# A decode attention kernel: value blocks move from the sync engine's transfer queue to ScalarE's

## The chip, the cores and the metric

The kernel runs on one core of a Trainium2 chip. A core has five engines that run their own instruction streams: TensorE (PE) for matrix products, VectorE (DVE), ScalarE (ACT), GpSimd (POOL) and the sync engine (SP). Transfers between the chip's main memory and the on-chip memory are started by an instruction on SP, ACT or POOL; the data is then moved by 16 DMA engines, which all three share. In the profile the queue that SP fills is called q1, the one that ACT fills q10, and the one that POOL fills q0.

The metric is device time in microseconds (us). Several runs of one kernel are timed without the profiler, and their median counts; one more execution is profiled.

## The reference

The computation is one decode step of a layer: attention with a cache and a small dense network, both on the same normalised input, summed with the input.

```python
xn = layernorm(x)                                   # x: 8 sequences x 512
q = (xn @ wq) -> 32 heads x 128                     # 4 query heads share one key/value head
scores = einsum("bhqd,bhkd->bhqk", q, k) * 128**-0.5   # k_cache: 8 x 8 heads x 8192 x 128
p = softmax(scores)
o = einsum("bhqk,bhkd->bhqd", p, v)                 # v_cache: 8 x 8 heads x 8192 x 128
out = x + o.reshape(8, 4096) @ wo                   # wo: 4096 x 512
        + mish(xn @ w1 + b1) @ w2                   # w1: 512 x 1792, w2: 1792 x 512
```

All numbers are 32-bit. The two caches hold 268 MB each, and every element is used once, so the caches make up nearly all of the 562 MB that the kernel reads.

## The kernel before, in words

The attention is cut into 32 units. A unit `j` is one sequence (`b = j % 8`) and two key/value heads (`m = j // 8`). It needs one block of keys and one block of values; each is 128 partitions x 16384 numbers, that is 64 KB in each partition and 8.39 MB in all. `load_unit` (line 135) starts such a transfer, and `load_q` (line 130) starts one of 2 MB with the part of `wq` that the next eight units need.

All blocks lie in one on-chip array `kv` with room for two and a half blocks: the value block at column 0, and two places for keys (`K_AT`) that overlap by half. Three rules follow for when a transfer may start, and a transfer's instruction waits for them on the engine that issues it:

- The keys of unit j+1 may come when the first half of the scores of unit j is done (`scores(..., 0)`, 32 matmuls of line 330), because that half has used up the columns that the next block overwrites.
- The values of unit j may come when the matmuls of `values(j-1)` (line 392) have used up the value block before.
- The values of the last unit go into a key place, and may come after the first half of the last unit's scores.

Within a unit PE does, in this order: the first half of the scores, the second half, two tiny transposes for the softmax's maximum, then `values(j-1)` of the unit before, and then `turn(j)` (lines 369 and 370), which re-arranges the exponentials for the next unit's `values`. DVE finishes `turn(j)` with transposes and sums (lines 374 and 380). ACT does one exponential per unit (line 361). Some units have more on PE between `values` and `turn`: `turn_act` in unit 2 (line 490), and `project` in units 5, 13 and 21 (lines 265 and 276), which makes the queries of the next group from `wq`. In units 7, 15 and 23 `spread` (line 301) does the rest of that.

Everything stands in the order in which the code writes it. SP issues nearly all transfers, first to last: keys of j+1, values of j, keys of j+2, and so on, with `wq` behind the values of units 4, 12 and 20. Two small gathers of early rows of `w2` (line 516, units 14 and 22) go by POOL's queue. After the loop SP starts `wo` in five transfers into the value place, 2 MB for each of `w_o[0]`, `w_o[1]`, `w_o[2]`, and 1 MB twice for `w_o[3]`, and then the rest of `w2` in four. Meanwhile PE does the last `values`, `outputs` (line 506), and `down` (line 553), and DVE and one last transfer end the kernel.

Of the kernel before, what the change touches and what calls it, by code (L numbers as in the profile page):

```python
# [35 lines left out]
NP = HKV // 2  # L36
# [5 lines left out]
UNITS = NP * B  # L42
# [34 lines left out]
def kernel(  # L77
# [12 lines left out]
    nc = tc.nc  # L90
# [7 lines left out]
    kv = const.tile([P, PLACES], F32, name="kv")  # L98
# [36 lines left out]
    def load_unit(src, j, at):  # L135
        m, b = divmod(j, B)
        lo = (b * HKV + 2 * m) * NH * G
        t = kv[:, at : at + ROW]
        nc.sync.dma_start(
            t,  # L140
            src[lo : lo + NB].rearrange("j p f -> (j p f)").rearrange("(p f) -> p f", p=P),
        )
        return t
# [18 lines left out]
    load_q(0)  # L162
    nc.scalar.dma_start(b1_sb, b1.rearrange("(g f) -> g f", g=B))
    k_t = {0: load_unit(kT, 0, V_AT)}
    w1_t = kv[:, W1_AT : W1_AT + 7168]

# [7 lines left out]
    for g in range(4):  # L174

        src = ident.rearrange("p (c d u g h) -> p d u g c h", c=2, d=2, u=2, g=4)
# [388 lines left out]
    key_weights(0)  # L565
    turn_x()
    k_t[1] = load_unit(kT, 1, K_AT[1])
    find_early()

# [3 lines left out]
    for j in range(UNITS):  # L573
# [3 lines left out]
        k = k_t.pop(j)  # L577
# [3 lines left out]
        if j == UNITS - 1:  # L581
            v_t[j] = load_unit(v, j, K_AT[0])
        elif j > 0:
            k_t[j + 1] = load_unit(kT, j + 1, K_AT[(j + 1) % 2])
# [30 lines left out]


    w_o = [kv[:, 4096 * m : 4096 * (m + 1)] for m in range(NP)]
    for m in range(NP):
        rows = wo[4 * m : 4 * (m + 1)].rearrange("u (k i) f -> (u k) (i f)", i=4)
        step = 4096 if m + 1 < NP else 2048  # L620
        for at in range(0, 4096, step):
            nc.sync.dma_start(w_o[m][:, at : at + step], rows[:, at : at + step])
    w2_rows = w2.rearrange("j p f -> (j p f)")[: P * FU * D].rearrange("(q f) -> q f", q=P)
    w2_t = []
    parts = ((0, 4), (4, 6), (6, 8), (8, 9))
# [65 lines left out]
```

## Time and profile before

| What | Value |
|---|---|
| median of 3 runs (lowest, highest) | 1308.74 us (1308.43, 1309.89) |
| profiled execution, its own time | 1308.41 us |
| span of that execution (first to last instruction) | 1306.6 us |
| PE busy | 995.1 us, 76% |
| DVE busy | 526.4 us, 40% |
| ACT busy | 41.4 us, 3% |
| bytes moved, mean rate over the span | 561.79 MB, 430 GB/s |
| mean granted TensorE clock | 0.878 |

The profiled execution's own time is 1.8 us more than its span, and 0.3 us less than the median. The rate is the sum over all 16 DMA engines. A row of a queue gives its packets, its megabytes, and the time that its packets took as a share of 16 engines' time. In the chain of waits each row is a start, a duration, and who was at work then. In the timeline the part in square brackets is how long the engine had been idle before the row, and for whom it waited.

### The profile page before, as it was taken

Reading aid. Unit: us, or ns where it says so; the run is one execution under the profiler, and the core shown is the slowest. Engines: PE = TensorE matmul, PEld = TensorE weight load, DVE = VectorE, ACT = ScalarE, POOL = GpSimd, SP = SyncE. Lnnn points to the kernel's source line nnn. Section 1 sums busy time; section 2 is a strip of 40 time slices with the busy share of each in tenths; the row PEclk is TensorE's granted clock in tenths of the full one; section 3 lists DMA queues with packets and bytes.
Section 4 is the critical chain, followed back from the end, with each engine's and each line's share of the span. In section 5 each row is a group of like instructions: output and inputs, shape, how many; then the busy total and the mean of one; then the engine's idle time right before and its main releaser. Section 6 shows DMA issues by size and latency. Waiting matters only on the chain.

```text
span 1306.6 us, 11259 instructions
## 1 busy us (share of the span) xinstructions
PE 995.1 (76%) x5046; PEld 336.1 (26%) x5046; DVE 526.4 (40%) x787; ACT 41.4 (3%) x90; POOL 7.8 (1%) x30
## 2 busy tenths in 40 slices
PE   5969977777977678777788777787776787776686
PEld 2324322222322222222222222222222222222221
DVE  4463344432444433244253444413444333444423
ACT  1000000000000000000000000000000000000000
POOL 1000000000000000000000000000000000000000
PEclk9988888798888789888898888798897998888888
DMA  9999999999999999999999999999999999999998
GB/s 405 442 424 440 428 436 432 432 434 434 430 436 426 441 424 444 420 446 418 446 418 446 420 444 422 442 426 438 424 440 430 434 432 434 430 436 428 439 424 356
DMA packets 11743, 561.79 MB, mean 430 GB/s; under 512 B 1464, under 2 KB 1600, under 8 KB 1992
## 3 DMA queue, kind: packets, MB, share of 16 engines
q1 hardware_dynamic: 11376, 559.75, 99.2%
q0 software_dynamic: 288, 1.31, 0.2%
q8 instruction: 39, 0.64, 0.2%
q14 instruction: 8, 0.07, 0.0%
q10 hardware_dynamic: 32, 0.02, 0.0%
HBM read 562.85 MB, written 0.07 MB: 431 GB/s over the span
## 4 chain that ended last, share of the span: by engine, by line
DMA 67%; PE 29%; DVE 3%; ACT 1%; issue 0%; DVEq 0%
DMA kv<-in_kT 34%; DMA kv<-in_v 31%; PE s L330 14%; PE o L392 10%; DMA kv<-in_w 2%; PE x L369 1%; PE x L301 1%; PE m L490 1%; DVE pt L380 1%; PE h L434 0%; PE h L265 0%; PE m L276 0%; ACT qr L304 0%; DVE ws L465 0%; DVE nm L342 0%
## 5 line engine op out<-in xcount | busy, mean ns | idle before, releaser
L330 PE MATMUL s<-kv,wk 128*64 128x512 f32 x2048 | 505.7, 656 | 160.3 <-DMA kv<-in_kT 160.3
L392 PE MATMUL o<-kv,pt 128*32 128x512 f32 x2048 | 264.3, 675 | 45.9 <-DMA kv<-in_v 36.3
L330 PEld LDWEIGHTS s<-kv,wk 128*64 128x64 f32 x2048 | 155.7, 152 | 482.6 <-issue 319.5
L380 DVE TENSOR_REDUCE pt<-tr 64x512 f32<-64x2048 f32 x64 | 241.3, 3771 | 1.5
L342 DVE TENSOR_REDUCE nm<-s 128x1 f32<-128x512 f32 x32 | 22.1, 692 | 335.8 <-PE s L330 335.8
L369 PE MATMUL x<-e,perm 128*128 128x512 f32 x256 | 129.7, 654 | 2.0 <-ACT qr L304 2.0
L392 PEld LDWEIGHTS o<-kv,pt 128*32 128x32 f32 x2048 | 69.0, 122 | 214.6 <-issue 166.3
L400 DVE TENSOR_SCALAR os<-o,isel 128x128 f32<-128x128 f32 x32 | 11.2, 351 | 261.5 <-PE o L392 261.5
L374 DVE STREAM_TRANSPOSE tr<-x 128x512 f32<-128x512 f32 x128 | 78.7, 673 | 0.0
L369 PEld LDWEIGHTS x<-e,perm 128*128 128x128 f32 x256 | 50.2, 206 | 77.9 <-issue 72.2
L313 DVE TENSOR_TENSOR wk<-qr,mask 128x512 f32<-128x512 f32 x64 | 62.9, 1025 | 16.2 <-ACT qr L304 16.2
L361 ACT ACTIVATE e<-s,nmx 128x512 f32<-128x512 f32 x32 | 22.0, 687 | 1076.1 <-DVE nmx L358 1076.1
L402 DVE SCALAR_TENSOR_TENSOR os<-o,isel,os 128x128 f32<-128x128 f32 x96 | 33.7, 351 | 3.4
L343 PE MATMUL m<-ident,nm 128*1 128x128 f32 x32 | 8.7, 273 | 30.5 <-DVE nm L342 30.5
L354 PE MATMUL m<-ident,nx 1*128 1x1 f32 x32 | 7.0, 219 | 24.0 <-DVE nx L350 24.0
L372 DVE RECIPROCAL rt<-m 128x8 f32<-128x8 f32 x32 | 6.6, 208 | 44.5 <-PE m L370 44.5
L409 PE MATMUL m<-hsel,os 128*128 128x8 f32 x64 | 12.6, 270 | 12.3 <-DVE rt L372 12.3
L301 PE MATMUL x<-wk,tr 128*128 128x512 f32 x16 | 13.1, 914 | 10.8 <-DVE wk L296 8.2
L363 DVE TENSOR_SCALAR lsel<-rsel,l 128x8 f32<-128x8 f32 x32 | 7.4, 231 | 30.0 <-ACT e L361 30.0
L343 PEld LDWEIGHTS m<-ident,nm 128*1 128x1 f32 x32 | 2.5, 79 | 58.7 <-DVE nm L342 58.7
L370 PEld LDWEIGHTS m<-lsel,ones 128*128 128x128 f32 x64 | 12.2, 190 | 15.5 <-issue 15.3
L347 DVE TENSOR_REDUCE nr<-m 1x4 f32<-1x64 f32 x64 | 10.9, 206 | 11.7 <-PE m L343 11.7
(114 smaller groups left out, 201.5 us busy)
## 6 DMA issues: line engine op xcount, KB each, us to landing
ws<-in_wq SPq DMA_DIRECT2D x4, 2048.0 KB, 33.8
kv<-in_wo SPq DMA_DIRECT2D x3, 2048.0 KB, 24.0
kv<-in_w SPq DMA_DIRECT2D x1, 3584.0 KB, 34.9
kv<-in_wo SPq DMA_DIRECT2D x2, 1024.0 KB, 30.4
kv<-in_w SPq DMA_DIRECT2D x1, 1024.0 KB, 32.5
kv<-in_w SPq DMA_DIRECT2D x2, 512.0 KB, 28.9
kv<-in_kT SPq DMA_DIRECT2D x32, 29.5
kv<-in_v SPq DMA_DIRECT2D x32, 30.6
```

What stands on the lines that cost most here:

```text
L301: nc.tensor.matmul(X[:, half], pick, r[:, i].rearrange("p i c -> p (i c)"), start=True, stop=True)
L313: nc.vector.tensor_mul(w[:, :, d], q[:, :, d].to_broadcast([P, DI, NH * G, REP]), mask[:, d * NH * G : (d + 1) * NH * G] .rearrange("p (o ...
L330: nc.tensor.matmul(S[64 * c : 64 * (c + 1), :], w[:, i].rearrange("p d k h -> p (d k h)"), kk[:, i, c, :], start=(part == 0 and n == 0), s ...
L342: nc.vector.tensor_reduce(nm, S, axis=AX.X, op=ALU.max, negate=True)
L361: nc.scalar.activation(e, S, AF.Exp, bias=nmx, accum_out=l)
L369: nc.tensor.matmul(X[:, g], perm[:, g], e, start=True, stop=True)
L374: nc.vector.transpose(tr.rearrange("p (l t) c -> p t l c", t=TL)[:, tl], X.rearrange("p g (t q l) -> p t l g q", t=TL, q=PP)[:, tl],)
L380: nc.vector.tensor_reduce(pt8[half, :, :, d * REP : (d + 1) * REP].rearrange("p c y h -> p y c h"), tr[half].rearrange("p y (g c h) -> p y ...
L392: nc.tensor.matmul(O[Q * q : Q * (q + 1), :], pt8[:, c, TL * l : TL * (l + 1), :].rearrange("p t h -> p (t h)"), vt[:, 512 * n : 512 * (n ...
L402: nc.vector.scalar_tensor_tensor(os, O[:, DH * i : DH * (i + 1)], isel[:, i : i + 1], os, op0=ALU.mult, op1=ALU.add)
L409: nc.tensor.matmul(M[:, 168 : 168 + H2], os, hsel, start=True, stop=True)
L490: nc.tensor.matmul(M[:, 256 + i * B : 256 + (i + 1) * B], w, bsel[:, :B], start=True, stop=True)
```

## The change

Values of units 0 to 30 are issued by ACT in place of SP. Keys, `wq`, the values of unit 31, `wo` and `w2` stay with SP. The first two blocks of `wo` become one transfer of 4 MB. No arithmetic is changed.

```diff
@@ load_unit
         t = kv[:, at : at + ROW]
-        nc.sync.dma_start(
+        (nc.scalar if src is v and j + 1 < UNITS else nc.sync).dma_start(
             t,
             src[lo : lo + NB].rearrange("j p f -> (j p f)").rearrange("(p f) -> p f", p=P),
         )
@@ after the loop over the units
     w_o = [kv[:, 4096 * m : 4096 * (m + 1)] for m in range(NP)]
-    for m in range(NP):
-        rows = wo[4 * m : 4 * (m + 1)].rearrange("u (k i) f -> (u k) (i f)", i=4)
-        step = 4096 if m + 1 < NP else 2048
-        for at in range(0, 4096, step):
-            nc.sync.dma_start(w_o[m][:, at : at + step], rows[:, at : at + step])
+    wo_rows = wo.rearrange("(m u) (k i) f -> m (u k) (i f)", m=NP, i=4)
+    nc.sync.dma_start(
+        kv[:, :8192].rearrange("p (m f) -> p m f", m=2),
+        wo_rows[:2].rearrange("m p f -> p m f"),
+    )
+    nc.sync.dma_start(w_o[2], wo_rows[2])
+    for at in (0, 2048):
+        nc.sync.dma_start(w_o[3][:, at : at + 2048], wo_rows[3, :, at : at + 2048])
```

On SP, units 2 to 5: `in_kT` are keys, `in_v` values, `in_wq` the query weights. Before:

```order
L139 DMA kv<-in_kT 128x16384
L139 DMA kv<-in_v 128x16384
L139 DMA kv<-in_kT 128x16384
L139 DMA kv<-in_v 128x16384
L133 DMA ws<-in_wq 128x4096
L139 DMA kv<-in_kT 128x16384
```

And now, from the keys of unit 1 on:

```order
L139 DMA kv<-in_kT 128x16384 x5
L133 DMA ws<-in_wq 128x4096
L139 DMA kv<-in_kT 128x16384 x8
L133 DMA ws<-in_wq 128x4096
L139 DMA kv<-in_kT 128x16384 x8
```

The values are gone from SP's stream, and `wq` now stands directly behind the keys of unit 5 and ahead of those of unit 6, with no block of values between.

On ACT, units 3 to 7: line 361 is a unit's exponential, line 273 a copy in `project`, line 304 one in `spread`. Before:

```order
L361 ACTIVATE e,l<-s,nmx 128x512 x5
L273 COPY e<-h 128x512 x2
L361 ACTIVATE e,l<-s,nmx 128x512 x2
L304 COPY qr<-x_69 128x512 x2
L361 ACTIVATE e,l<-s,nmx 128x512 x6
```

And now:

```order
L361 ACTIVATE e,l<-s,nmx 128x512
L139 DMA kv<-in_v 128x16384
L361 ACTIVATE e,l<-s,nmx 128x512
L139 DMA kv<-in_v 128x16384
L273 COPY e<-h 128x512 x2
L361 ACTIVATE e,l<-s,nmx 128x512
L139 DMA kv<-in_v 128x16384
L361 ACTIVATE e,l<-s,nmx 128x512
L139 DMA kv<-in_v 128x16384
L304 COPY qr<-x_69 128x512 x2
```

Each unit's values now stand behind that unit's exponential and ahead of the copies of `project` and `spread`.

On SP, the end. Before:

```order
L139 DMA kv<-in_v 128x16384 x2
L622 DMA kv<-in_wo 128x4096 x3
L622 DMA kv<-in_wo 128x2048 x2
L628 DMA kv<-in_w 128x2048
L628 DMA kv<-in_w 128x1024 x2
L628 DMA kv<-in_w 128x512
```

And now:

```order
L139 DMA kv<-in_v 128x16384
L619 DMA kv<-in_wo 128x2x4096
L623 DMA kv<-in_wo 128x4096
L625 DMA kv<-in_wo 128x2048 x2
L631 DMA kv<-in_w 128x2048
L631 DMA kv<-in_w 128x1024 x2
L631 DMA kv<-in_w 128x512
```

Of the two last blocks of values one is left on SP, and two transfers of `wo` have become one.

## The prediction

> **What bounds the kernel now.** I read the page first: queues, then chain.
>
> ```profile
> q1 hardware_dynamic: 11376, 559.75, 99.2%
> q0 software_dynamic: 288, 1.31, 0.2%
> ...
> q10 hardware_dynamic: 32, 0.02, 0.0%
> ...
> DMA 67%; PE 29%; DVE 3%; ACT 1%; issue 0%; DVEq 0%
> ```
>
> SP's queue is busy for 99.2% of the time of 16 engines, nearly everything goes through it, and ACT's (q10) is all but unused. The same view for 40 us of the middle:
>
> ```profile
> DMA packets 298, 17.33 MB, mean 433 GB/s; under 512 B 32, under 2 KB 32, under 8 KB 32
> ...
> q1 hardware_dynamic: 296, 17.30, 100.1%
> ```
>
> 296 - 32 = 264 packets carry 17.30 MB, so a packet is 65.5 KB: one partition's row of a block, eight on each engine. 264 packets in 40 us on 16 engines make 2.42 us each, and a block **D = 8 x 2.42 = 19.4 us**. The queue has no gap here. Next the chain at the end:
>
> ```profile
> 1200.40 8.60 PE s L330 x32
> ...
> 1209.02 30.10 DMA kv<-in_kT
> ...
> 1239.16 9.70 PE s L330 x32
> ...
> 1248.88 28.96 DMA kv<-in_v
> ...
> 1277.85 24.61 DMA kv<-in_w
> ...
> 1302.51 0.62 PE h L553 x16
> ```
>
> Keys of unit 31 land at 1239.16, a period of 38.76 us after those of unit 30: exactly two blocks. The chain goes through key loads that were issued about 9 us after a landing and landed 30 us later: 10 us in line, 19.4 us moving. The stream of bytes is the bound, and 10 us of queued work keeps it unbroken.
>
> **Issue times: nothing to win.** The waits of SP's queue and of ACT:
>
> ```profile
> SPq L139 <- PE s L330: 315.7, 32, 19.3
> ...
> SPq L139 <- PE o L392: 253.2, 30, 12.1
> ```
>
> ```profile
> ACT e L361 <- DVE nmx L358: 1076.1, 31, 40.7
> ```
>
> SP waits for PE: for a score half before keys, for `values` before values. PE does these in the order in which SP asks, so none of SP's transfers is held up by its neighbour's wait, and ACT will wait for the same PE instructions. ACT is idle for 1076 us before its exponentials. Behind its new wait stand the next exponential, whose scores PE does after that `values`, and the copies of `project` and `spread`, also later on PE. So the wait on ACT costs nothing; 31 issues of 0.33 us (SP's rows below) hide in that idle time, and without it would cost 10 us. The first values come behind unit 0's exponential:
>
> ```profile
> 29.55 0.33 SPq L139 DMA_DIRECT2D kv<-in_kT  x1
> 44.99 0.33 SPq L139 DMA_DIRECT2D kv<-in_v  x1
> ```
>
> ```profile
> 48.56 0.69 ACT L361 ACTIVATE e<-s,nmx 128x512 f32<-128x512 f32 x1
> ```
>
> That is some 4.3 us later (49.25 against 44.99), while unit 1's keys, asked for at 29.55 behind `wq`, the first keys and `w1`, are still moving: nothing, and 4.3 us if they had already landed.
>
> **What does change: two rings.** Before, a block got all engines until it was through. Now keys and values wait in two queues at once. The one place before where two queues were long in use is POOL's gather in unit 14, 0.92 MB. Its landing, and three stretches of 7.5 us from 565.5 us on:
>
> ```profile
> q0 software_dynamic: 144, 0.92, 6.5%
> ...
> ws<-in_w,idx POOLq DMA_INDIRECT x1, 29.3
> ```
>
> ```profile
> q1 hardware_dynamic: 61, 2.95, 91.0%
> q0 software_dynamic: 61, 0.41, 13.1%
> ```
>
> ```profile
> q1 hardware_dynamic: 46, 3.01, 92.9%
> q0 software_dynamic: 45, 0.25, 7.9%
> ```
>
> ```profile
> q1 hardware_dynamic: 52, 3.41, 104.9%
> q0 software_dynamic: 34, 0.23, 7.3%
> ```
>
> The gather's 16 KB rows, 0.61 us each at a block's rate, are up to eight on an engine: 4.9 us if drained at one go. They trickle through all three stretches instead. Alternating one for one with 64 KB rows takes 8 x (2.42 + 0.61) = 24.2 us, and with some 4 us of start that is the 29.3 us seen. So I take it that the engines alternate between queues row by row, and two blocks then get half the rate each.
>
> The Trainium skill (DMA: Bandwidth & Descriptors, Queues, rings and completion order) says that an engine goes round its queues but drains a whole packet, typically 9 to 17 descriptors, before it switches. By that a block's eight rows on an engine could go as one piece; the stretches above speak against it, and the first rival asks what it would do.
>
> **One period with sharing.** T is the landing of a unit's keys, x the us of the value block that have moved by then. PE's rows in the last unit, all matmuls of the values, PE's clock just after a wait for keys (0.50, the third number from the right), a score half that followed no wait, and SP's last issue:
>
> ```profile
> 1239.16 16.53 PE L330 MATMUL s<-kv,wk 128*64 128x512 f32 x64 [6.14 <-DMA kv<-in_kT]
> ...
> 1258.52 8.51 PE L392 MATMUL o<-kv,pt 128*32 128x512 f32 x64 [0.79 <-DMA kv<-in_v]
> ```
>
> ```profile
> L392 PE MATMUL o<-kv,pt 128*32 128x512 f32 x2048 | 264.3, 675 | 45.9 <-DMA kv<-in_v 36.3
> ```
>
> ```profile
> 690.00:692.00 2.00, 2.00 (x6) 0.70 (x8) 2.00 (x1) 0.00 (x0) 0.00 (x0) 0.50 1.21 524
> ```
>
> ```profile
> 652.40 7.04 PE s L330 x32
> ```
>
> ```profile
> 1303.93 0.35 SPq L652 DMA_DIRECT2D out<-os  x1
> ```
>
> The first half takes 9.2 us (8.60 and 9.70 above). From an issue to its first byte I take 1.6 us: the last transfer was issued at 1303.93, and all of it is over by the span's end, 1306.6, so it is under 2.7. The next keys then start at T + 10.8. PE is ready for `values` at T + 18.6 (1258.52 - 0.79 - 1239.16), which take 8.3 us on average (264.3 / 32).
>
> - Values alone until T + 10.8, then shared: they land at T + 10.8 + 2 x (8.6 - x) = T + 28 - 2x.
> - Their successor starts 9.9 us later. The keys then have 0.9 + x left, and share that: the next x is 0.9 + x. It climbs until the landing meets PE's T + 18.6, at x = 4.7; past that, x' = 38.8 - 27.3 - x with `values` at full clock (7.1 us), so about 5 or 6. Where PE has not idled before the keys its clock is full and the half takes 7.0 us (652.40): the next keys start 2.2 us sooner, and x falls by 1.3 instead.
>
> So x wanders between 0 and 6; I take the middle, **x = 3**. No gap arises in an ordinary unit: the values last past T + 10.8 for x under 8.6. But the cushion, 10 us before, is halved.
>
> **Gaps in long units.** SP's timeline around the issue of unit 2's values and unit 4's keys; the size of a `wq` transfer; and PE's first score matmuls of unit 6, behind `project`:
>
> ```profile
> 123.61 0.33 SPq L139 DMA_DIRECT2D kv<-in_v  x1
> 147.01 0.33 SPq L139 DMA_DIRECT2D kv<-in_kT  x1
> ```
>
> ```profile
> ws<-in_wq SPq DMA_DIRECT2D x4, 2048.0 KB, 33.8
> ```
>
> ```profile
> 255.70 1.12 PE L330 MATMUL s<-kv,wk 128*64 128x512 f32 x2 [4.38 <-DMA kv<-in_kT]
> ```
>
> In unit 2 PE needs 23.4 us from one issue to the other (`turn_act`). All that the engines hold then is that block and what is left of unit 3's keys, which by the sharing is x again: 19.4 + x, so a gap of 4.0 - x, **1.0 us** (0 to 4). In unit 5 `wq` stands ahead of unit 6's keys. Its rows are 16 KB (2048 KB on 128 partitions), eight per engine, and alternate with the 64 KB rows of the values (25% slower: with x = 3, 16.4 x 3.03 / 2.42 = 20.5 us), so the keys start at T + 21. The values' successor starts at 20.5 + 8.3 + 1.6 = T + 30.4; 10 us of keys are left, shared, so they land at T + 50.4, and x is 10 by then: 1.4 over the 8.6 allowed, a gap of 1.4. (PE itself is on time: it had 4.4 us to spare after `project`, and the keys now come later.) The same in units 13 and 21: 3 x 1.4 = **4.2 us**. Sum I = 5.2, from 0 (sharing less even) to 9: a landing waits for the slowest of 16 engines, each up to a packet (2.4 us) off.
>
> **The tail.**
>
> ```profile
> 1281.04 9.19 PE L392 MATMUL o<-kv,pt 128*32 128x512 f32 x64 [9.57 <-DVE pt L380]
> ...
> 1302.51 1.03 PE L553 MATMUL h<-kv,aT 128*8 128x128 f32 x24 [0.48 <-DMA kv<-in_w]
> ```
>
> `values(30)` ends at 1267.03 (1258.52 + 8.51). The rest up to 1306.6 is 39.6 us of PE, DVE and ACT in series, of which only 0.48 waits for a transfer. PE and the stream end together; the slack is half a microsecond. Now the last values share with the block of unit 31. T becomes 1239.1 + I + x, as x us of values went first; `values(30)` ends 28 - 2x + 8.3 later, and the end 39.1 after that: 1314.5 + I - x, against 1306.6 + I for the bytes. At x = 3 it is **+4.9 us**; at 0, +7.9. From x = 4.7 on `values(30)` ends at T + 18.6 + 7.1, and the end is 1303.9 + I + x: +2.0 at 4.7, the least, and +3.3 at 6. The merged `wo` is asked for up to a quarter of `values` (2.1 us) later, behind unit 31's values, which have some 8 us to go: nothing, or 2.1 us without that cover.
>
> Sum on the profiled execution: 1308.4 + 5.2 + 4.9 = **1318.5 us**, its own range 1310.4 (0 and 2.0) to 1325.3 (9 and 7.9). The median lies 0.3 above that execution, which I leave in the rounding.
>
> **The rivals.** For the second, the rate (last number, GB/s) of the stretch in which the tail's bytes come:
>
> ```profile
> 1277.90:1303.20 25.30, 19.66 (x214) 6.44 (x218) 5.70 (x11) 0.58 (x1) 0.00 (x0) 0.85 0.95 397
> ```
>
> - Blocks drained in order of issue (12%): an engine that has begun a block's eight rows finishes them before it looks at the other queue. Then landings, gaps and tail are as before, and so is the time, 1308.7. For it: q1 and q10 were never seen side by side under load. Against: the gather's stretches.
> - Faster (8%): two queues close what q1 leaves open. 99.2 + 0.2 + 0.2% leaves about 0.4%, 5 us, and the start and end hold most of it; the last 25.3 us run at 397 GB/s in place of 433, worth 2.1 us. That gives 1305 to 1306.5. Against: 100.1% in the middle.
> - Sharing with a hidden tail (10%): x ends near 4.7 (+2.0), and `values(31)` finds the full clock, 7.1 us in place of the 9.19 above, which takes those 2.1 us back. Then the gaps alone remain, 1308.4 + 5.2 = 1313.6. For it: x tends to 4.7. Against: `values(31)` waits 9.57 us for DVE in either kernel, and starts cold.
>
> **How the numbers follow.** The forecast has 70%. Some 0.2% (2.6 us) is what a measurement can tell from no change. Forecast and third rival are slower (80%); the first is the same (12%), the second faster (8%). The range runs from 1308, to take in the first rival, to 1326, just past the likeliest one's own end; what it leaves out is the second rival and a tail longer than any x here gives.
>
> **What would show it.** q10 should carry half of the bytes; keys and values should both take well over 30 us from issue to landing; PE's wait for values should grow from 36 us; gaps of 1 to 2 us in the DMA should follow unit 2 and units 5, 13, 21; and at the end PE should no longer wait for `w2`, with `values(30)` ending about 8 to 10 us later. Landings as before in a row would prove the forecast wrong at the sharing; a higher rate than 433 GB/s in the middle would prove the second rival.

## The result and the profile after

The changed kernel takes 1330.7 us (median of four runs, 1327.95 to 1334.29) where the kernel before, beside it, takes 1308.59 (1308.29 to 1309.89). The ratio is 1.017, with a 95% interval from 1.0158 to 1.0183. It is slower, as forecast, but by 22.1 us in place of 10, and beyond the range's end at 1326. The profiled execution is the longest of the four: 1334.29, with a span of 1332.5, 25.9 more than before. All rows of the kernel after come from it.

The page of the kernel after: bytes, queues, the two groups of matmuls, and the median us from issue to landing (these last two rows from the DMA view).

```profile
DMA packets 11728, 561.80 MB, mean 422 GB/s; under 512 B 1448, under 2 KB 1584, under 8 KB 1976
...
q1 hardware_dynamic: 6896, 299.70, 52.7%
q10 hardware_dynamic: 4496, 260.07, 45.4%
...
L330 PE MATMUL s<-kv,wk 128*64 128x512 f32 x2048 | 491.6, 641 | 149.0 <-DMA kv<-in_kT 148.8
L392 PE MATMUL o<-kv,pt 128*32 128x512 f32 x2048 | 265.3, 677 | 103.5 <-DMA kv<-in_v 93.9
...
kv<-in_kT SPq DMA_DIRECT2D x32, 29.8
kv<-in_v ACTq DMA_DIRECT2D x31, 29.5
```

Nearly half of the bytes have moved to q10. The same bytes come at 422 GB/s in place of 430. PE waits 57.6 us more for values (93.9 against 36.3), and 11.5 less for keys (148.8 against 160.3). Keys and values still take only 29.8 and 29.5 us from issue to landing (29.5 and 30.6 before).

**Where the time went.** Busy time by engine in 40 to 1280 us, with the granted clock, the DMA share and the rate as the last three numbers; before, then after:

```profile
40.00:1280.00 1240.00, 950.75 (x4732) 319.85 (x4728) 507.31 (x725) 34.94 (x80) 2.12 (x2) 0.87 1.00 432
```

```profile
40.00:1280.00 1240.00, 919.83 (x4638) 311.86 (x4636) 495.03 (x707) 34.16 (x78) 2.12 (x2) 0.86 0.99 425
```

The middle is 7 GB/s slower, which is 1240 x 7 / 432 = 20 us of the stream's time. In stretches of 100 us of the kernel after, the rate (before: 429 to 436 in every such stretch) is:

| stretch from, us | 40 | 140 | 240 | 340 | 440 | 540 | 640 | 740 | 840 | 940 | 1040 | 1140 |
|---|---|---|---|---|---|---|---|---|---|---|---|---|
| before, GB/s | 436 | 429 | 434 | 432 | 434 | 429 | 435 | 432 | 431 | 434 | 433 | 432 |
| after, GB/s | 419 | 423 | 427 | 430 | 429 | 429 | 431 | 410 | 430 | 423 | 422 | 429 |
| stream time lost, us | 3.9 | 1.4 | 1.6 | 0.5 | 1.2 | 0.0 | 0.9 | 5.1 | 0.2 | 2.5 | 2.5 | 0.7 |

The losses sum to 20.5 us. They are spread over the kernel, most of them in places where the prediction had none. The deepest holes in the same view of the kernel after:

```profile
110.00:120.00 10.00, 10.00 (x48) 3.11 (x46) 0.00 (x0) 0.00 (x0) 0.00 (x0) 0.94 0.84 334
815.00:821.00 6.00, 6.00 (x42) 2.08 (x35) 2.22 (x5) 0.00 (x0) 0.00 (x0) 1.00 0.55 188
1000.00:1005.00 5.00, 5.00 (x26) 1.73 (x24) 3.39 (x2) 0.00 (x0) 0.00 (x0) 1.00 0.77 275
```

PE is busy through all three while the DMA engines are not full: for most of each, the transfers that would fill them are not yet asked for. None of the three is one that the prediction named. PE's rows near the first and the third:

```profile
131.27 9.59 PE L490 MATMUL m<-bsel,ws 128*128 128x8 f32 x42
...
983.79 2.07 PE L301 MATMUL x<-wk,tr 128*128 128x512 f32 x2 [0.67 <-ACT qr L304]
...
993.63 13.95 PE L330 MATMUL s<-kv,wk 128*64 128x512 f32 x64
```

The first hole ends before `turn_act` (line 490) has begun. The gap that the prediction named lies behind `turn_act`, at 150 to 160 us, and left the engines idle for 0.8 us. The third follows the `spread` of unit 23 (line 301), a unit that the prediction did not count among the long ones: PE turned to the keys of unit 24 at 993.63, 8 us after they had landed. Only the second lies in an ordinary unit.

Read packet by packet, the 16 engines stood idle for 12.6 us each between 40 and 1280 us, and for 0.0 in the kernel before. The other part of the loss is in rows that took longer than the usual 2.42 us: the first rows of the blocks add up to 9 us over that on each engine, most of it within 5 us after an idle spell. Why they take longer is not shown.

**One hole, followed.** PE's wait ahead of the hole at 815, and ACT's issue after it, from the timeline:

```profile
808.73 9.87 PE L392 MATMUL o<-kv,pt 128*32 128x512 f32 x64 [13.77 <-DMA kv<-in_v]
...
818.67 0.34 ACTq L139 DMA_DIRECT2D kv<-in_v  x1
```

The DMA view of 815.2 to 819.5, and then of 819.5 to 820.5:

```profile
DMA packets 12, 0.07 MB, mean 15 GB/s; under 512 B 11, under 2 KB 11, under 8 KB 11
...
q1 hardware_dynamic: 12, 0.07, 3.7%
```

```profile
q10 hardware_dynamic: 15, 0.98, 290.1%
```

The values came 13.77 us late for PE, after sharing the engines with the keys. `values` then took 9.87 us where it takes 7.07 without a wait before it; the granted clock was 0.50 from 808.7 to 814 us and 1.00 from 816 on. In that time the keys ran out, and the next values were asked for only at 818.67. In the 4.3 us of the first of these views, which take in the issue, only one row begins. The second view holds 15 first rows at 290.1% of 16 engines' 1 us, which makes 3.09 us each. So a cushion that had been 10 us was gone in an ordinary unit.

The last 4.5 us of PE's wait were for a single engine. The DMA view of 802 to 804, and then of 804 to 808.5:

```profile
q1 hardware_dynamic: 15, 0.98, 113.3%
q10 hardware_dynamic: 16, 0.07, 8.0%
```

```profile
q1 hardware_dynamic: 30, 1.97, 100.8%
q10 hardware_dynamic: 1, 0.00, 0.0%
```

Each engine ends its part of a block with one small packet. Fifteen of those of the values, and the last value row (0.07 MB), begin before 804. The sixteenth begins at 808.34, among 30 rows of keys, and PE starts at 808.73.

**The end.** PE's timeline, after:

```profile
1268.39 15.63 PE L330 MATMUL s<-kv,wk 128*64 128x512 f32 x64 [11.93 <-DMA kv<-in_kT]
...
1285.98 7.07 PE L392 MATMUL o<-kv,pt 128*32 128x512 f32 x64
...
1307.07 9.87 PE L392 MATMUL o<-kv,pt 128*32 128x512 f32 x64 [9.57 <-DVE pt L380]
...
1327.53 2.15 PE L553 MATMUL h<-kv,aT 128*8 128x128 f32 x72
```

The keys of unit 31 land 29.2 us later than before (1268.39 against 1239.16). From there the end is PE's chain: `values(30)` follows with no wait and ends at 1293.05, the kernel 39.45 us behind it. PE no longer waits for `w2` (line 553). Read packet by packet, the last row of the stream ends 24.1 us later than before, 1.8 us less than the kernel; 20.5 of these 24.1 are lost by 1240 us, as the table shows, and the rest behind that.

### The profile page after: what moved, and what is told of

The parts are those of the page before. It is cut to its first block, busy times and chain, and to the rows that moved or that the text cites. A ratio compares the mean times of both kernels' runs of the same rounds, so it can differ in the third digit from the quotient of the medians.

```text
span 1332.5 us, 11258 instructions
## 1 busy us (share of the span) xinstructions
PE 980.1 (74%) x5046; PEld 333.9 (25%) x5046; DVE 526.3 (40%) x787; ACT 41.4 (3%) x90; POOL 7.8 (1%) x30
## 4 chain that ended last, share of the span: by engine, by line
DMA 67%; PE 29%; DVE 2%; ACT 0%; issue 0%; SPq 0%; ACTq 0%
DMA kv<-in_v 37%; DMA kv<-in_kT 30%; PE o L392 14%; PE s L330 12%; PE x L369 1%; PE m L490 1%; PE x L301 1%; DVE pt L380 1%; PE x L506 1%; PE h L265 0%; PE m L276 0%; DVE tr L374 0%; ACT qr L304 0%; DVE nm L342 0%; PE h L553 0%
## 5 line engine op out<-in xcount | busy, mean ns | idle before, releaser
L330 PE MATMUL s<-kv,wk 128*64 128x512 f32 x2048 | 491.6, 641 | 149.0 <-DMA kv<-in_kT 148.8
L392 PE MATMUL o<-kv,pt 128*32 128x512 f32 x2048 | 265.3, 677 | 103.5 <-DMA kv<-in_v 93.9
L342 DVE TENSOR_REDUCE nm<-s 128x1 f32<-128x512 f32 x32 | 22.1, 692 | 308.8 <-PE s L330 308.8
L347 DVE TENSOR_REDUCE nr<-m 1x4 f32<-1x64 f32 x64 | 11.0, 207 | 11.6 <-PE m L343 11.6
## 6 DMA issues: line engine op xcount, KB each, us to landing
kv<-in_w SPq DMA_DIRECT2D x1, 1024.0 KB, 30.6
kv<-in_kT SPq DMA_DIRECT2D x32, 29.8
```

What stands on the lines that cost most here:

```text
L330: nc.tensor.matmul(S[64 * c : 64 * (c + 1), :], w[:, i].rearrange("p d k h -> p (d k h)"), kk[:, i, c, :], start=(part == 0 and n == 0), s ...
L342: nc.vector.tensor_reduce(nm, S, axis=AX.X, op=ALU.max, negate=True)
L392: nc.tensor.matmul(O[Q * q : Q * (q + 1), :], pt8[:, c, TL * l : TL * (l + 1), :].rearrange("p t h -> p (t h)"), vt[:, 512 * n : 512 * (n ...
```

## The experiments

The first four take the change apart. Each diff is against the changed kernel.

**Only the merged `wo`.** Values go back to SP's queue.

```diff
-        (nc.scalar if src is v and j + 1 < UNITS else nc.sync).dma_start(
+        nc.sync.dma_start(
```

> All transfers stay on the sync engine's queue; only the first two blocks of wo come as one transfer. Theory (the whole loss is two queues taking turns): the stream is one queue again, without gaps, so 1308.6 +- 1 us. Rival (part of the loss is the merged wo, asked for later and landing in one piece at the end): 1311 us or more, with PE's outputs waiting for wo.

Measured: 1308.21 us, ratio 0.9998 (0.9988 to 1.0007). The merge costs nothing.

**One queue, but ACT's.** All large transfers (`wq`, keys, values, `w1`, `wo`, `w2`) are issued by ACT, in their old order.

```diff
-        (nc.scalar if src is v and j + 1 < UNITS else nc.sync).dma_start(
+        nc.scalar.dma_start(
...
-        nc.sync.dma_start(ws, rows[m])
+        nc.scalar.dma_start(ws, rows[m])
```

> All large transfers (keys, values, wq, w1, wo, w2) are issued by ScalarE, none but the output by the sync engine; wo merged as in the change. Theory (turns between two queues, not the issuing engine): one queue, in the order of before, 1308.6 us, at most 1310. Rival (a transfer that waits on ScalarE, behind and ahead of its exponentials, is issued late): 1325 us or more, with transfers issued later than the matmuls that free their place.

Measured: 1308.74 us, ratio 1.0001 (0.9992 to 1.0011). Its page and its waits:

```profile
q10 hardware_dynamic: 11248, 559.71, 99.2%
```

```profile
ACT e L361 <- DVE nmx L358: 1076.8, 31, 41.8
```

The whole stream went through ACT's queue, with ACT's waits for PE on every block, and took the time of before. ACT's wait for its exponentials is unchanged too (1076.1 before). So neither ACT as the issuer nor q10 itself costs anything. What costs is that two queues are filled at once.

**By units.** Values go by ACT in units 0 to 23 only, then in units 24 to 30 only.

```diff
-        (nc.scalar if src is v and j + 1 < UNITS else nc.sync).dma_start(
+        (nc.scalar if src is v and j < 24 else nc.sync).dma_start(
```

> Values of units 0 to 23 by ScalarE's queue, those of units 24 to 31 by the sync engine's; wo merged. Theory now (gaps at nearly every hand-over because a block's completion packet also waits its turn behind a row of the other queue, 2.4 us; plus an exposed tail of some 2 to 5 us): the gaps of units 0 to 23 remain, the tail is as before: 1324 us (1320 to 1327). The theory of the prediction (gaps in units 2, 5, 13, 21 only, then the tail): 1313 to 1315 us, the rest of the loss in the tail. If the tail were all of it: 1308.6 us.

```diff
-        (nc.scalar if src is v and j + 1 < UNITS else nc.sync).dma_start(
+        (nc.scalar if src is v and 24 <= j and j + 1 < UNITS else nc.sync).dma_start(
```

> Values of units 24 to 30 alone by ScalarE's queue; wo merged. Theory now: gaps of about 0.7 us in each of seven units and the exposed tail, 1308.6 + 6 = 1315 us (1312 to 1318). The theory of the prediction: no gaps here, the tail alone, 1312 to 1314 us. If the loss were all in the tail: 1330 us; if all in the long units: 1308.6 us.

Measured: 1324.43 us (1323.26 to 1334.19), ratio 1.0145 (1.0105 to 1.0185), for units 0 to 23, and 1315.63 (1313.14 to 1329.32), ratio 1.0066 (1.0042 to 1.009), for units 24 to 30. The two excesses, 16.0 and 7.2 us over 1308.47, add up to 23.2, and the full change has 22.1; with ranges of 11 and 16 us that agreement is rough. The first kernel has the old tail, so its 16 us (13.7 at the lower end of the interval) are lost in the stream alone, for which the prediction had 5.2. The windows of the kernel before, and then of each of the two, in the same order:

```profile
40.00:980.00 940.00, 730.76 (x3620) 247.75 (x3618) 386.98 (x555) 28.13 (x63) 2.12 (x2) 0.87 1.00 433
980.00:1280.00 300.00, 219.99 (x1114) 72.10 (x1110) 120.32 (x170) 6.81 (x17) 0.00 (x0) 0.87 1.00 431
```

```profile
40.00:980.00 940.00, 688.65 (x3560) 238.21 (x3556) 374.64 (x545) 26.97 (x61) 2.12 (x2) 0.86 1.00 427
980.00:1280.00 300.00, 231.70 (x1155) 76.58 (x1158) 122.06 (x169) 7.98 (x19) 0.00 (x0) 0.88 1.00 431
```

```profile
40.00:980.00 940.00, 735.70 (x3630) 250.06 (x3628) 387.05 (x555) 28.17 (x63) 2.13 (x2) 0.87 1.00 433
980.00:1280.00 300.00, 227.72 (x1112) 72.98 (x1108) 112.17 (x166) 6.81 (x17) 0.00 (x0) 0.85 1.00 429
```

The rate falls in the units whose values went by ACT, and only there. With units 24 to 30 alone it falls little, and PE's timeline of that kernel shows the tail:

```profile
1243.52 15.65 PE L330 MATMUL s<-kv,wk 128*64 128x512 f32 x64 [3.71 <-DMA kv<-in_kT]
...
1265.39 9.85 PE L392 MATMUL o<-kv,pt 128*32 128x512 f32 x64 [4.19 <-DMA kv<-in_v]
```

In the prediction's terms T = 1243.52, 4.4 later than before. The values land 21.9 us after T, and 28 - 2x = 21.9 gives x = 3.05, with I = 4.4 - 3.05 = 1.3 us of gaps. Read packet by packet, x was 3.6 and the engines stood idle for 0.8 us between 40 and 1280 us, so the gaps of 0.7 us in each of seven units that I expected were not there. The end comes at 1314.4, 39.2 behind the end of `values(30)`. That is the prediction's tail at its x = 3, to a microsecond and a half (`values` took 9.85 in place of 8.3).

**Shorter rows.** If the engines take turns row by row, what a transfer loses to a turn is a row's time. The next kernels cut each block of keys and values into R rows per partition of 64/R KB. The caches are stored in the order in which they are read, so the on-chip contents and the sums are the same. For each R there is a kernel with one queue (with `wo` as before) and one with two.

```diff
-            t,
-            src[lo : lo + NB].rearrange("j p f -> (j p f)").rearrange("(p f) -> p f", p=P),
+            t.rearrange("p (h f) -> p h f", h=R),
+            src[lo : lo + NB].rearrange("j p f -> (j p f)").rearrange("(h p f) -> p h f", h=R, p=P),
```

> The kernel before (one queue) with each block of keys and values stored so that a partition's part comes as two rows of 32 KB instead of one of 64 KB; same bytes, same numbers. Control for the next run. Both theories: still one queue without gaps; rows of 16 KB took 0.615 us where a quarter of a 64 KB row takes 0.605, some 0.009 us per row, so 1313 us (1309 to 1316).

> The kernel before (one queue) with four rows of 16 KB per partition and block. Control for the next run: 1323 us (1318 to 1328), by the same 0.009 us per row.

> The changed kernel with the same rows of 32 KB on both queues. Theory now (the loss comes from waiting one turn, and a turn is one row of the other queue, for a block's completion and its first row): half the turn, so the loss against its control falls from 22 us to about 10 us (8 to 15). Rival (two queues at once move bytes more slowly, or lose time at each switch): as many bytes and twice the switches, so the loss stays at 22 us or grows to 40.

> The changed kernel with rows of 16 KB on both queues. Theory now: a turn is a quarter of before, 0.6 us, and what is left is the sharing itself and the tail, the loss of the prediction without turns: 7 us (5 to 12) against its control. Rival: 22 us or, with four times the switches, up to 80 us.

| row | one queue, us | two queues, us | loss, us |
|---|---|---|---|
| 64 KB | 1308.59 | 1330.7 (1327.95 to 1334.29) | 22.1 |
| 32 KB | 1313.2, ratio 1.0036 (1.0022 to 1.005) | 1331.16 (1324.67 to 1337.78), ratio 1.0163 (1.0115 to 1.0211) | 18.0 |
| 16 KB | 1322.89, ratio 1.011 (1.0093 to 1.0126) | 1334.83 (1328.67 to 1337.4), ratio 1.0193 (1.0162 to 1.0224) | 11.9 |

The one-queue times came as expected. Of the two others, 16 KB lies at the upper end of what was expected, and 32 KB misses: 18.0 where 10 (8 to 15) was written. The loss does fall with the row, so a part of it belongs to the length of a turn. But 11.9 us stay at a quarter of the length, so another part does not. Ranges of 9 to 13 us in the two-queue kernels make the single differences rough: by the intervals of the ratios the loss is 10 to 23 us at 32 KB, which alone is not clear of 22.1, and 7 to 15 us at 16 KB, which is. Idle time of the engines, read packet by packet, was 12.6 us with 64 KB rows and 6.6 with 16 KB. One rival is not excluded: the cut itself slows the stream by 14.5 us, some 0.45 us a unit, which leaves PE more time in each. Windows of the two 16 KB kernels, one queue and then two:

```profile
40.00:1280.00 1240.00, 957.26 (x4712) 321.59 (x4711) 496.81 (x714) 34.98 (x80) 2.12 (x2) 0.85 1.01 428
```

```profile
40.00:1280.00 1240.00, 903.51 (x4636) 310.59 (x4634) 495.14 (x707) 34.17 (x78) 2.12 (x2) 0.86 1.00 424
```

1240 x 4 / 428 = 11.6 us, good to 3 us since the rates are rounded: here too most of the loss is in the rate of the middle.

**Rows of unequal length.** If a turn is one row whatever its length, the queue with rows of half the length gets a third of the bytes while both are full. Two kernels with two queues: 32 KB rows for keys alone, then for values alone.

```diff
+        cut = 2 if src is kT else 1
...
-            t,
-            src[lo : lo + NB].rearrange("j p f -> (j p f)").rearrange("(p f) -> p f", p=P),
+            t.rearrange("p (h f) -> p h f", h=cut),
+            src[lo : lo + NB].rearrange("j p f -> (j p f)").rearrange("(h p f) -> p h f", h=cut, p=P),
```

> The changed kernel with the keys stored as two rows of 32 KB per partition and the values as one of 64 KB; same bytes. Theory (the engines take turns row by row, whatever a row's length): while both queues hold work the keys get one third of the rate and the values two thirds; the values pass the keys, the queue of values runs dry until PE has new scores, and the engines idle in every unit: 1390 us (1350 to 1430), keys over 33 us from issue to landing, values under 28. Rival (the engines share by bytes, or drain a block before they switch): the time of the change, 1331 us and some 2 for the shorter rows, with landings as in the change, 29.8 and 29.5 us.

> The opposite: keys in rows of 64 KB, values in two rows of 32 KB. Theory: the keys get two thirds; the values are passed, PE waits for them with the next keys already there and their successors not yet allowed, and the engines hold one block alone for long: 1500 us (1430 to 1560), keys under 28 us from issue to landing, values over 36. Rival: 1333 us, as in the change.

Measured: 1386.05 us, ratio 1.059 (1.0559 to 1.062), and 1470.24, ratio 1.1233 (1.12 to 1.1266). Issues with their landings and PE's waits, keys cut:

```profile
kv<-in_kT SPq DMA_DIRECT2D x32, 8192.0 KB, 30.9
...
kv<-in_v ACTq DMA_DIRECT2D x31, 27.6
```

```profile
PE s L331 <- DMA kv<-in_kT: 306.1, 31, 18.5
...
PE o L393 <- DMA kv<-in_v: 2.0, 2, 1.0
```

Values cut:

```profile
kv<-in_v ACTq DMA_DIRECT2D x31, 8192.0 KB, 36.3
...
kv<-in_kT SPq DMA_DIRECT2D x32, 28.7
```

```profile
PE o L393 <- DMA kv<-in_v: 350.7, 26, 25.8
...
PE s L331 <- DMA kv<-in_kT: 33.2, 7, 7.2
```

The side with the shorter rows comes late, and nearly all of PE's waiting is for it (306.1 us against 2.0, and 350.7 against 33.2); with both sides cut alike, the time was 1331.16. Sharing by bytes, or a block drained in one piece, would not care which side is cut, and neither can give 55 and 139 us for it. Both times lie within the bounds written. Three of the four landings were within the bounds written or 0.7 us off; the keys, when cut, took 30.9 us where over 33 was expected.

The Trainium skill (DMA: Bandwidth & Descriptors, Queues, rings and completion order) lets an engine drain a packet of some 9 to 17 descriptors before it turns to another queue. Here each 64 KB or 32 KB row was a turn of its own. Whether such a row is one descriptor or a packet of several, no run here shows.

## Why the prediction was right, and where it failed

**Right: the mechanism.** The engines alternate row by row. A window of the kernel after, 640 to 680 us, in which both queues are full:

```profile
q10 hardware_dynamic: 146, 8.52, 50.1%
q1 hardware_dynamic: 145, 8.45, 49.0%
```

The turns are equal, and the unequal rows confirm that it is turns that are equal, not bytes. The first rival (blocks drained in order) falls with this, and the second (faster) with the rate: no stretch in the table exceeds its own before. That the issues on ACT and the merged `wo` cost nothing was shown by the runs of each alone. The Trainium skill (DMA: Bandwidth & Descriptors, Issuing engines are not separate DMA queues) says that starting transfers on several engines at once saves only the time that it takes to start them. The 425 GB/s against 432 agree that no rate is won, and add that some can be lost.

**Right: the tail's form.** `values(30)` plus a fixed chain: 39.45 and 39.2 us here, 39.1 forecast. With few gaps before it (units 24 to 30 alone) it cost what was written for x = 3. In the full change T moved by 29.2: the 20.5 us lost by 1240 us, and the 8.7 us of values that had moved by T, read packet by packet. `values` found no wait, and by T + 18.6 + 7.1 + 39.1 the end is 1333.2; it was 1332.5. The tail's term was 4.9 of the sum; 25.9 less 20.5 leaves 5.4. That is near for an x of 8.7 where 3 was taken; by its own formula the term would be 6.0.

**The signs.** q10 carries nearly half of the bytes, PE's wait for values grew from 36.3 to 93.9 us, and PE no longer waits for `w2`. `values(30)` ends 26.0 us later (1293.05 against 1267.03), not 8 to 10, because the gaps were larger. The landings stayed at 29.8 and 29.5 us, where the prediction wanted well over 30 as a sign of the sharing. That sign was badly chosen: before, a block stood some 10 us in line and moved for 19.4; now it begins sooner and moves more slowly, and both come to about 30.

**Failed: the sum of gaps, I = 5.2 (0 to 9).** It measured 20 us. Two of the named places were there: behind `turn_act` in unit 2 (140 to 240 us: 1.4 lost, 1.0 forecast) and behind the `wq` of unit 5 (240 to 340: 1.6 lost, 1.4 forecast). The second agrees by luck: the forecast starts from x = 3 at the landing of unit 5's keys, and x was 8.1. Units 13 and 21, where x was 2.5 and 0.0, lost nothing (540 to 640: 0.0; 840 to 940: 0.2), so the step on `wq` is not borne out. Some 17 of the 20.5 us lie elsewhere. The third rival, which kept the forecast's gaps and hid the tail, falls with that: 16 us are lost in the stream with units 0 to 23 alone.

The step that failed is "So x wanders between 0 and 6", and with it "No gap arises in an ordinary unit: the values last past T + 10.8 for x under 8.6". The bound was about right. The range of x was not, because T, the landing, comes a row later than the last of the keys.

*When a transfer is over.* At 808.73 PE started only behind the sixteenth small packet. The same at the end: the DMA view around the landing of the keys of unit 31, 1263.3 to 1265.5, then 1265.5 to 1268.4:

```profile
DMA packets 30, 0.98 MB, mean 447 GB/s; under 512 B 15, under 2 KB 15, under 8 KB 15
...
q10 hardware_dynamic: 15, 0.98, 103.4%
q1 hardware_dynamic: 15, 0.00, 0.4%
```

```profile
DMA packets 23, 1.44 MB, mean 497 GB/s; under 512 B 1, under 2 KB 1, under 8 KB 1
...
q10 hardware_dynamic: 22, 1.44, 115.0%
q1 hardware_dynamic: 1, 0.00, 0.0%
```

In the first stretch no key row begins any more; 15 small packets of q1 pass between 15 value rows. The sixteenth comes later, alone, among 22 value rows, at 1267.94, and PE starts at 1268.39. The last key row had ended at 1265.53, 2.41 us before that packet. Read packet by packet, 28 of the 31 landings of keys after unit 0 show the same 2.4 us (2.6 at most) between a block's last row and its last small packet, and the other three none; of the values, 21 of the 29 that could be told apart show it too. Before, the median is 0.1. With 32 KB rows on both queues the typical delay is 1.21 us, and with 16 KB rows 0.61. Each is the time of one row of the other queue: the small packet waits for a turn. The prediction had "a landing waits for the slowest of 16 engines" only in the bounds of I.

*What it does to x.* The values go on moving in those 2.4 us. Counted at the end of the last key row, x runs from -1.5 to 7.6 in units 2 to 31, with a mean of 2.9: close to what the prediction had, and below its bound. Counted at T, it runs from -1.5 to 10.0, with a mean of 5.0, and is above 6 in 12 of the 30 units. The units with x of 5.7 or more, without unit 5, where `wq` fills the engines, and the last:

| unit | 2 | 6 | 25 | 27 | 29 | 4 | 7 | 8 | 22 | 26 | 28 | 30 |
|---|---|---|---|---|---|---|---|---|---|---|---|---|
| x at the last key row's end, us | 7.6 | 6.4 | 4.7 | 7.4 | 6.3 | 3.3 | 3.9 | 3.8 | 3.7 | 3.9 | 3.8 | 4.1 |
| x at T, us | 10.0 | 8.8 | 7.2 | 9.8 | 8.7 | 5.7 | 6.3 | 6.2 | 6.0 | 6.3 | 6.2 | 6.5 |
| idle until the next landing, us per engine | 2.3 | 1.4 | 0.5 | 0.7 | 0.3 | 0.0 | 0.0 | 0.1 | 0.0 | 0.0 | 0.0 | 0.0 |

The gaps are where x at T is 7.2 or more. They make up 5.1 of the 12.6 us of idle time. The hole at 815 has 4.3: there x was small (0.4), the values came late as shown above, and the request for their successors with them. Another 2.1 us lie in units 3 (behind `turn_act`), 14 (with POOL's gather) and 24 (behind `spread`).

*When a transfer begins.* I took 1.6 us from issue to first byte, from a transfer issued at the end, when the engines were free. ACT's issue in unit 30, and the DMA view of 1252.1 to 1255.5, then of 1255.5 to 1258:

```profile
1252.08 0.33 ACTq L139 DMA_DIRECT2D kv<-in_v  x1
```

```profile
q1 hardware_dynamic: 21, 1.38, 93.4%
```

```profile
q10 hardware_dynamic: 16, 1.05, 96.8%
```

q10 shows no packet in the first 3.4 us after the issue. But 21 key rows began in that time, so no engine stood idle for it. After the issue at 818.67, with the engines empty, 15 rows had begun by 820.5, 1.8 us later (the view of 819.5 to 820.5 above). That is the case that makes a gap, and for it the 1.6 us was near.

**Open.** That the late landing makes the gaps at high x is read from the packets and fits the shorter rows; no run takes the delay away and leaves the rest. Why the first row behind an idle spell takes longer, and how one engine came to lag a round behind in unit 19, is not shown. The loss depends on the state in which a unit starts: the four runs spread over 6 us, units 24 to 30 alone left the engines idle for 0.8 us, and in the full change the rate from 940 to 1240 us lost 5.7.

## What to carry to other kernels

A stream that is bound by bytes, and whose blocks are needed in a known order, belongs in one queue in that order: a second queue lets two blocks share, and a landing that comes late delays the next request. A cushion should be counted from the moment at which the consumer knows of the landing, not from the end of the last row: with two full queues that was one row of the other queue later here. Where two queues do run side by side, their shares are set by row lengths, so the more urgent one must not have the shorter rows.

## What the runs showed of the hardware that was not expected

- A block's small last packet takes its turn behind one row of the other queue: 2.41 us after the last key row with 64 KB rows (1265.53 to 1267.94), 1.21 with 32 KB, 0.61 with 16 KB, and a median of 0.1 with one queue.
- While the other queue kept the engines busy, a new block's first row came more than 3.4 us after its issue (1252.08); with the engines empty, 15 rows had begun after 1.8 us (818.67).
- First rows behind an idle spell took longer: 3.09 us in place of 2.42 behind the hole at 815.
- Turns go by rows, not bytes: halving one side's rows alone cost 55 us (keys) or 139 us (values) over halving both.
- A row costs little by itself: 32 KB rows put 512 more on each engine and cost 4.8 us (1313.2 - 1308.44), 16 KB rows 1536 more and 14.5 us (1322.89 - 1308.44), 0.009 us each in both.
